# Two token tiles transposed by the DMA, their first two products interleaved, and z spread by a row in DRAM

## The chip, the cores and the metric

The kernel runs on one core of a Trainium2 chip. The time is that of one execution on the device, in microseconds; what is given for a kernel is the median of several executions. An execution is also recorded by the profiler once: that record has a span (first to last instruction), engine busy times, and waits. PE is the matmul engine, DVE the vector engine, ACT the activation engine, POOL the general one; SP issues most DMAs.

## What is computed

For 2048 tokens of width D = 640 the output is a gate between a linear attention with 32 heads of width 20 (feature maps: softmax of a projection and of its negative) and a SwiGLU feed-forward net of width 1728.

```python
qkv = x @ wqkv                                   # q, k, v: 32 heads of 20
pq, pk = q @ w_phi, k @ w_phi                    # per head, 20 x 20
phi_q = concat(softmax(pq), softmax(-pq))        # 40 features a head
phi_k = concat(softmax(pk), softmax(-pk))
kv  = einsum("bhsf,bhsd->bhfd", phi_k, v)        # sums over all tokens
z   = einsum("bhsf->bhf", phi_k)
o   = (phi_q @ kv) / (phi_q @ z + 1e-6)
a   = o @ wo
b   = (silu(x @ w_gate) * (x @ w_up)) @ w_down
g   = sigmoid((x * gate_w).sum(-1))
out = g * a + (1 - g) * b
```

## The kernel before, in words

Tokens are cut into 16 tiles of 128 (`NT`), and these into four blocks of four tiles. Every matmul that contracts over D has five steps c = 0..4 of 128 rows. The stages are written as small functions, and a list of their names and arguments, `ORDER` (line 31), gives the order in which they are issued. Each engine runs its own instructions in that order; the class `_Tracker` (line 45) puts a semaphore wait ahead of an instruction wherever it reads or overwrites what another engine or a DMA has still in hand. So a stage's place in the list sets its place on every engine's queue.

The letters of the list:

- `H` (`warm`): matmuls of a tile of ones, with no use but to keep PE active; `NWARM` to a stage.
- `L` (`load_ffn_weights`): the DMAs of the feed-forward and output weights, on SP.
- `X` (`xpose`): the transpose of one token tile, by five PE transposes and a DVE copy from PSUM. It is done for the tiles t < `NPE`, that `load_x` (line 352) brings as they are; the others arrive transposed by the DMA (`dma_start_transpose`, SP). `G`: the gate's weight as an extra column of `wvg`.
- `V` (`vtile`): v of one tile, ten matmuls (five c, two halves of 320 columns) with the weight rows `wvg`, which come in five DMAs, one for each c; ACT copies the result into `v1r` and the gate's sum into `svec`.
- `W` (`wxpose`): PE transposes of one row block of the k weights (`wkn`), copied by DVE into `wT`. `Y` (`w_blocks`): `wbd`, the small matrices w_phi laid out in blocks, made by POOL and DVE. `M` and `R` (`premult`, lines up to 522): k and q weights multiplied by w_phi, six matmuls for each row block, into `wqk`.
- `K` (`ktile`): pk of a tile, ten matmuls; two exponentials on ACT, sums and reciprocals on DVE, the product on POOL into `ekr`. `E` (`kvtile`): eleven matmuls of `ekr` with v, summed over all tiles in PSUM banks 6 and 7. `I` and `N` begin and end that time: between them three PSUM pairs go round (`next_pair`), outside them four. `N` also runs `kv_finish` (line 525).
- `Z` (`z_broadcast`, line 541): z reaches all partitions. `kv_finish` makes `dz`, a diagonal matrix holding z for each of 11 groups of 120; matmuls with ones spread it to 128 partitions, and ACT copies it into `zb`. `J`: the gates.
- `Q` (`qtile`): pq of a tile and its exponentials `eq`; `A` sums them (`qz`); `B` (`qden`) multiplies them by `zb` (`ez`); `C` (`qscale`) sums that, makes the factors `qc`, and has POOL scale `eq` into `ph`, which a transposing DMA on SP brings to `phiT`.
- `O` (`oitem`, parts 0 to 2 of a block): `phiT` with `kvsb`, matmuls with 64 columns of weights; ACT copies to `oT`.
- `F` (`fitem`, 14 parts of a block): ten matmuls of 512 columns, tanh and a copy on ACT, a step on DVE and one on POOL into `hT`. `D` (`ditem`): 38 matmuls of 320 columns for the output of one tile, from `hT` and `oT`; ACT scales into `osb` and the store goes out. The last tile is done in two halves (line 665).

All of the loads stand ahead of the list, on the queues of SP and ACT (lines 361 to 376). On each queue DMAs are issued one after the other.

Of the kernel before, what the change touches and what calls it, by code (L numbers as in the profile page):

```python
# [6 lines left out]
P = 128  # L7
S_TOK = 2048
D = 640
H = 32  # L10
# [2 lines left out]
NT = S_TOK // P  # L13
NB = 4
NCH = 11
NPE = 4
NV = 6
NWARM = 3
FP = 120 * NCH
FK = FP + 8  # L20
ACTF = mybir.ActivationFunctionType
# [7 lines left out]


ORDER = """
L H0 H1 H2 G H3 H4 H5 X0 H6 H7 V0 X1 X2 X3 V1 Y W0 W1 W2 V2 W3 W4 V3 M0 M1 M2 M3 M4 K0 I V4 K1 R0
K2 V5 K3 E0 R2 V6 K4 E1 K5 R4 E2 K6 E3 V7 K7 R1 E4 V8 E5 K8 K9 V9 F0.0 V10 E6 K10 E7 F0.1 E8 V11
K11 E9 K12 V12 K13 R3 E10 K14 V13 E11 K15 Q0 V14 F0.2 V15 E12 E13 J E14 E15 N Q1 F0.3 Q2 A0 Z A1
B0 A2 F0.4 F0.5 F0.6 C0 B1 F0.7 F1.0 Q3 C1 A3 F0.8 F1.1 B2 F1.2 C2 F0.9 F0.10 B3 Q4 F1.3 A4 Q5 C3
F1.4 F0.11 T F0.12 B4 Q6 C4 A5 F1.5 F1.6 B5 F1.7 O0.0 A6 O0.1 F1.8 B6 Q7 A7 F0.13 O0.2 C5 F1.9
F1.10 Q8 C6 A8 B7 D0.0 D0.1 D0.2 Q9 F1.11 C7 D0.3 F2.0 F2.1 F2.2 F1.12 B8 O1.0 O1.1 O1.2 A9 C8
Q10 F2.3 F1.13 Q11 A10 F2.4 B9 F2.5 C9 A11 B10 Q12 D1.0 F2.6 C10 F2.7 D1.1 F2.8 B11 F2.9 F2.10
Q13 A12 C11 D1.2 Q14 D1.3 O2.0 A13 B12 A14 F3.0 B13 F3.1 F3.2 O2.1 C12 C13 F3.3 F3.4 B14 F2.11
Q15 F2.12 A15 F3.5 F2.13 C14 F3.6 O2.2 B15 F3.7 C15 F3.8 D2.0 F3.9 F3.10 F3.11 F3.12 D2.1 O3.0  # L40
O3.1 O3.2 F3.13 D2.2 D3.0 D3.1 D2.3 D3.2 D3.3
"""


# [143 lines left out]
def _build(nc, A_x, A_wqkv, A_w_phi, A_wo, B_x, B_w_gate, B_w_up, B_w_down, gate_w, out):  # L188
# [5 lines left out]
    def sb(name, shape, dtype):  # L194
        t = nc.alloc_sbuf_tensor(name, list(shape), dtype)
        tr.reg(t, "sbuf", nc.lookup_mloc(t).addr)
        return t
# [14 lines left out]
    hmask = sb("hmask", [P, 3], F32)  # L212
    zt = sb("zt", [P, NCH, 3], F32)
    zf = sb("zf", [P, NCH], F32)
    dz = sb("dz", [P, NCH, 120], BF16)
    zb = sb("zb", [P, FP], BF16)
    svec = sb("svec", [P, NT], F32)
    g2 = sb("g2", [P, NT], F32)
# [22 lines left out]
    def at(name, shape, dtype, rel):  # L241
        n = mybir.dt.size(dtype)
        for s in shape[1:]:
            n *= s
        assert rel + n <= SLAB, (name, rel + n, SLAB)
        t = nc.alloc_sbuf_tensor_at(name, list(shape), dtype, offset=sbase + rel)
        tr.reg(t, "sbuf", sbase + rel)
        return t
# [8 lines left out]
    wph = at("wph", [P, 5, DH], BF16, 28480)  # L257
    bmask = at("bmask", [P, 5, 8], BF16, 28736)
    gwr = at("gwr", [P, P], BF16, 28864)

    ps = nc.alloc_psum_tensor("ps", [P, 8 * 512], F32)
    tr.reg(ps, "psum", 0)

    def bank(b, c0, c1, r0=0, r1=P):
        return ps[r0:r1, b * 512 + c0:b * 512 + c1]
# [66 lines left out]
    def dma(e, dst, src, transpose=False):  # L332
        eo = tr.eng[e]

        def fn():
            if transpose:
                return eo.dma_start_transpose(dst, src)
            return eo.dma_start(dst, src)  # L338
        rd = [src] if src.tensor.name in tr.base else []
        wr = [dst] if dst.tensor.name in tr.base else []  # L340
        return run(e, fn, rd, wr, dma=True)
# [10 lines left out]
    def load_x(t, e="sp"):  # L352
        if t < NPE:
            dma(e, xs[:, t, :], x2[t * P:(t + 1) * P, :])
        else:
            dma("sp", xT[:, t, :, :], x2[t * P:(t + 1) * P, :], transpose=True)

    def load_rows(e, dst, c, c0):
        dma(e, dst, A_wqkv[c * P:(c + 1) * P, c0:c0 + D])

    dma("act", gwr[0:5, :], bass.AP(gate_w.tensor, gate_w.offset, [[P, 5], [1, P]]))
    load_x(0)
    for c in range(5):
        load_rows("sp" if c % 2 else "act", wvg[:, c, 0:D], c, 2 * D)
    load_x(1)
    load_x(2, "act")
    load_x(3)
    dma("act", wph[:, :, :], A_w_phi.rearrange("h e f -> (h e) f").rearrange("(c p) f -> p c f", p=P))
    for c in range(5):
        load_rows("sp", wkn[:, c, :], c, D)  # L370
    for t in range(4, 7):
# [49 lines left out]
    def next_pair():  # L421
        r = ring["i"] % ring["n"]
        ring["i"] += 1
        return r
# [16 lines left out]
        pr = next_pair()  # L441
        mm([(bank(2 * pr, 0, P), ones[:, :], ones[:, :], True, True, False)] * NWARM)

    def vtile(t):
        pr = next_pair()
        pairs = [(bank(2 * pr + hb, 0, 320 + hb), xT[:, t, c, :], wvg[:, c, 320 * hb:640 + hb - 320 * (1 - hb)],
                  c == 0, c == 4, False) for c in range(5) for hb in range(2)]
        if t == 0:
            for c in range(5):
                mm(pairs[2 * c:2 * c + 2])  # L450
        else:
            mm(pairs)
        i = halves(pr).rearrange("p b (h d) -> p b h d", d=DH)
        o = v1v[:, t % NV, 0:H, 0:DH].rearrange("p (b h) d -> p b h d", b=2)
        copy("act", o, i)
        copy("act", svec[:, t:t + 1], bank(2 * pr + 1, 320, 321))

    def head_exps(pr, dst):
        i = halves(pr).rearrange("p b (h d) -> p b h d", d=DH)
# [28 lines left out]
    def kvtile(t):  # L488
# [6 lines left out]
                          t == 0 and jj == 0, t == NT - 1, True))  # L495
        mm(pairs)

    def wxpose(m):
        pr = next_pair()
        o = bankbf(2 * pr, 640)  # L500
        transposes([(o[:, c * P:(c + 1) * P], wkn[:, m, c * P:(c + 1) * P]) for c in range(5)])
        copy("dve", wT[:, m, :, :].rearrange("p c k -> p (c k)"), o)

# [11 lines left out]
    def premult(which, m):  # L515
        pr = next_pair()
        pairs = []
        for i, (hb, c, c0, c1, off) in enumerate(BANDS):
            o = bank(2 * pr + hb, c0 - 320 * hb, c1 - 320 * hb)
            pairs.append((o, (wT if which else wTq)[:, m, c, :], wbd[:, c, off:off + c1 - c0], i in (0, 3), i in (2, 5), True))  # L520
        mm(pairs)
        copy("dve" if which and m % 2 == 0 else "act", wqk[:, which, m, :].rearrange("p (b c) -> p b c", b=2), halves(pr))


    def kv_finish():
        for bk, j0, j1 in ((KV0, 0, 8), (KV0 + 1, 8, NCH)):
            n = j1 - j0
            i = bank(bk, 0, 63 * n, 0, 120).rearrange("p (j h d) -> p j h d", h=3, d=DH + 1)
            tt("dve", zt[0:120, j0:j1, :], i[:, :, :, DH],
               hmask[0:120, :].unsqueeze(1).to_broadcast([120, n, 3]), ALU.mult)  # L530
        reduce(zf[0:120, :], zt[0:120, :, :])
        tt("dve", dz[0:120, :, :], ident[0:120, 0:120].unsqueeze(1).to_broadcast([120, NCH, 120]),
           zf[0:120, :].unsqueeze(2).to_broadcast([120, NCH, 120]), ALU.mult)
        for bk, j0, j1 in ((KV0, 0, 8), (KV0 + 1, 8, NCH)):
            n = j1 - j0
            i = bank(bk, 0, 63 * n, 0, 120).rearrange("p (j h d) -> p j h d", h=3, d=DH + 1)
            for hh in range(3):
                tt("dve", kvsb[0:120, j0:j1, 20 * hh:20 * hh + 20], i[:, :, hh, 0:DH],
                   hmask[0:120, hh:hh + 1].unsqueeze(1).to_broadcast([120, n, DH]), ALU.mult)

    def z_broadcast():
        pr = next_pair()
        dzf = dz[0:120, :, :].rearrange("p j c -> p (j c)")
        mm([(bank(2 * pr, 0, 480), ones[0:120, :], dzf[:, 0:480], True, True, False),
            (bank(2 * pr + 1, 0, 480), ones[0:120, :], dzf[:, 480:960], True, True, False)])
        copy("act", zb[:, 0:960].rearrange("p (b c) -> p b c", b=2), halves(pr, 480))
        pr = next_pair()
        mm([(bank(2 * pr, 0, 360), ones[0:120, :], dzf[:, 960:FP], True, True, False)])
        copy("act", zb[:, 960:FP], bank(2 * pr, 0, 360))

    def gates():
        tsc(svec[:, :], svec[:, :], 60.0, None, ALU.min, ALU.bypass)
# [95 lines left out]
    def ditem(bt, u):  # L648
        buf = bt % 2
        t = 4 * bt + u  # L650
        pr = next_pair()
        tok = slice(P * u, P * u + P)
        ls = [(hT[:, buf, k, tok], wd[:, k, :]) for k in range(13)]
        ls += [(hT[0:104, buf, 13, tok], wd[0:104, 13, :])]
        ls += [(oT[:, buf, m, tok], wog[:, m, :]) for m in range(5)]
        n = len(ls)
        half = [[(bank(2 * pr + hb, 0, 320), l, r[:, 320 * hb:320 * hb + 320], i == 0, i == n - 1, False)
                 for i, (l, r) in enumerate(ls)] for hb in range(2)]
        o = osb[:, t % 4, :]
        if t < NT - 1:  # L660
            mm([p for ab in zip(*half) for p in ab])
            actop(o.rearrange("p (b c) -> p b c", b=2), halves(pr), ACTF.Copy, omg[:, t:t + 1])
            out_evs.append(dma("sp", out2[t * P:(t + 1) * P, :], o))
            return
        for hb in range(2):
            mm(half[hb])
            c = slice(320 * hb, 320 * hb + 320)
            actop(o[:, c], bank(2 * pr + hb, 0, 320), ACTF.Copy, omg[:, t:t + 1])
            out_evs.append(dma("sp", out2[t * P:(t + 1) * P, c], o[:, c]))


    def kv_begin():
# [2 lines left out]
    def kv_end():  # L675
# [1 line left out]
        ring["n"] = 4  # L677

    ops = {
        "H": lambda i: warm(), "X": xpose, "G": gcol, "V": vtile, "W": wxpose,  # L680
        "M": lambda m: premult(1, m), "R": lambda m: premult(0, m),
        "K": ktile, "E": kvtile, "L": load_ffn_weights, "T": tail_weights, "J": gates,
        "Y": w_blocks, "I": kv_begin, "N": kv_end, "Z": z_broadcast,
# [54 lines left out]
```

## Time and profile before

| what | value |
|---|---|
| median of 8 runs | 295.83 us (295.43 to 298.15) |
| the profiled execution's own time | 295.9 us |
| its span | 294.2 us |
| PE busy | 289.1 us, 98% of the span |
| DVE, ACT, POOL busy | 171.7, 148.6, 158.0 us |
| granted PE clock | full over the whole span |
| DMA | 21.28 MB, mean 72 GB/s |

The profile's lines name an engine, a line of the code, an operation with what it writes and reads (out<-in), its shape, and how many there are. In the timeline the first two numbers are the start and the time taken, both in us, and a bracket tells how long the engine had been idle and what ended that. Since every matmul passes through one helper, all have line 284, and are told apart by their tiles. PEld is the loading of weights into PE. SPq and ACTq are the queues that issue DMAs.

### The profile page before, as it was taken

What the parts mean: (1) busy time and instruction counts of PE and PEld (TensorE: products, weight loads), DVE (VectorE), ACT (ScalarE), POOL (GpSimd) and SP (SyncE); (2) the same over time, 40 slices, a digit from 0 to 9 for tenths busy, and PEclk for the clock granted to TensorE, in tenths of its full rate; (3) what the DMA queues carried; (4) which work ended last, traced back from release to release, by engine and by line L of the source; (5) the groups of instructions that cost most, each with busy time, mean ns of one, the idle gap of its engine ahead of it and who ended that gap; (6) DMA issues with size and microseconds to landing.
All of it is one profiled execution on the core that took longest, in us unless ns stands there. A gap on an engine that the chain in (4) does not pass through costs nothing.

```text
span 294.2 us, 4908 instructions
## 1 busy us (share of the span) xinstructions
PE 289.1 (98%) x1981; PEld 174.5 (59%) x1981; DVE 171.7 (58%) x250; ACT 148.6 (51%) x252; POOL 158.0 (54%) x118
## 2 busy tenths in 40 slices
PE   7999999999999999999999999999999999999996
PEld 5777766766444544357764456647544455657774
DVE  1558775585979989997042777539259893100000
ACT  1378865784746655852235862353356644262112
POOL 8709887794268878955025384544056976410000
PEclk9999999999999999999999999999999999999999
DMA  7967899500002222203203021230302223000101
GB/s 215 210 115 114 232 359 362 113 3 0 2 0 49 51 49 49 49 2 76 69 22 72 3 49 25 49 71 2 94 0 49 51 49 71 3 22 25 45 22 48
DMA packets 45993, 21.28 MB, mean 72 GB/s; under 512 B 35794, under 2 KB 45970, under 8 KB 45970
## 3 DMA queue, kind: packets, MB, share of 16 engines
q1 hardware_dynamic: 44728, 20.27, 29.0%
q10 hardware_dynamic: 1242, 0.68, 0.8%
q8 instruction: 16, 0.26, 0.4%
q14 instruction: 7, 0.06, 0.1%
HBM read 9.78 MB, written 2.62 MB: 42 GB/s over the span
## 4 chain that ended last, share of the span: by engine, by line
PE 90%; DVE 5%; DMA 2%; ACTq 1%; ACT 1%; issue 0%
PE ps L284 90%; DMA xs<-in_A_x_dram 2%; DVE qw L323 1%; DVE hT L316 1%; PE ps L296 1%; ACTq L338 1%; DVE qw L316 1%; DVE qm L583 1%; DVE qz L323 0%; DVE ez L312 0%; ACT hT L302 0%; DVE qd L326 0%; DVE qc L588 0%; DVE qd L312 0%; ACT osb L302 0%
## 5 line engine op out<-in xcount | busy, mean ns | idle before, releaser
L312 POOL TENSOR_TENSOR hT<-hT,us 128x512 bf16<-128x512 bf16 (+1 forms) x56 | 69.8, 1258 | 62.5 <-DVE hT L316 62.5
L316 DVE SCALAR_TENSOR_TENSOR hT<-hT,ps 128x512 bf16<-128x512 bf16 (+1 forms) x56 | 37.6, 682 | 61.8 <-ACT hT L302 51.0
L284 PE MATMUL ps<-xT,wg 128*128 128x512 bf16 x260 | 64.7, 380 | 0.3 <-DVE hT L316 0.2
L284 PE MATMUL ps<-xT,wu 128*128 128x512 bf16 x260 | 64.6, 380 | 0.0
L284 PE MATMUL ps<-wd,hT 128*128 128x320 bf16 x448 | 63.7, 300 | 0.0
L302 ACT ACTIVATE hT<-ps 128x512 bf16<-128x512 f32 (+2 forms) x60 | 35.8, 596 | 47.0 <-PE ps L284 45.1
L284 PEld LDWEIGHTS ps<-wd,hT 128*128 128x128 bf16 x448 | 43.8, 98 | 17.8
L312 POOL TENSOR_TENSOR ph<-eq,qc 128x1320 bf16<-128x1320 bf16 x16 | 39.3, 2457 | 27.1 <-DVE qc L588 27.1
L284 PE MATMUL ps<-wqk,xT 128*128 128x320 bf16 x320 | 48.4, 299 | 0.1
L312 POOL TENSOR_TENSOR ekr<-ekr,krec 128x1280 bf16<-128x1280 bf16 x16 | 37.3, 2358 | 16.1 <-DVE krec L326 13.9
L284 PEld LDWEIGHTS ps<-xT,wu 128*128 128x128 bf16 x260 | 25.4, 98 | 30.7
L302 ACT ACTIVATE osb<-ps,omg 128x640 bf16<-128x640 f32 (+1 forms) x17 | 12.9, 762 | 58.5 <-PE ps L284 58.5
L284 PEld LDWEIGHTS ps<-xT,wg 128*128 128x128 bf16 x260 | 24.9, 98 | 29.5 <-issue 1.2
L284 PEld LDWEIGHTS ps<-wqk,xT 128*128 128x128 bf16 x320 | 30.4, 98 | 14.0 <-ACT us L302 0.5
L302 ACT ACTIVATE us<-ps 128x512 bf16<-128x512 f32 (+1 forms) x56 | 33.2, 594 | 0.6 <-POOL hT L312 0.5
L323 DVE TENSOR_REDUCE ksum<-ekr 128x64 f32<-128x1280 bf16 x16 | 23.5, 1468 | 14.7 <-ACT ekr L302 14.7
L302 ACT ACTIVATE eq<-ps 128x640 bf16<-128x640 f32 x32 | 22.5, 703 | 15.7 <-POOL ph L312 11.3
L302 ACT ACTIVATE ekr<-ps 128x640 bf16<-128x640 f32 x32 | 22.4, 704 | 8.4 <-PE ps L284 7.9
L284 PE MATMUL ps<-wvg,xT 128*128 128x320 bf16 (+1 forms) x160 | 25.8, 308 | 0.4 <-DMA wvg<-in_A_wqkv_dram 0.4
L284 PE MATMUL ps<-wog,oT 128*128 128x320 bf16 x160 | 24.5, 299 | 0.0
L323 DVE TENSOR_REDUCE qz<-eq 128x64 f32<-128x1280 bf16 x16 | 23.6, 1479 | 1.3 <-ACT eq L302 1.3
L323 DVE TENSOR_REDUCE qw<-ez 128x64 f32<-128x1280 bf16 x16 | 23.6, 1476 | 0.0
(71 smaller groups left out, 196.5 us busy)
## 6 DMA issues: line engine op xcount, KB each, us to landing
out_dram<-osb SPq DMA_DIRECT2D x15, 160.0 KB, 1.8
wd<-in_B_w_down_dram SPq DMA_DIRECT2D x1, 2080.0 KB, 16.9
wkn<-in_A_wqkv_dram SPq DMA_DIRECT2D x5, 160.0 KB, 5.5
wg<-in_B_w_gate_dram SPq DMA_DIRECT2D x1, 800.0 KB, 7.7
wu<-in_B_w_up_dram SPq DMA_DIRECT2D x1, 800.0 KB, 10.5
wog<-in_A_wo_dram SPq DMA_DIRECT2D x2, 375.0 KB, 6.7
wg<-in_B_w_gate_dram SPq DMA_DIRECT2D x1, 720.0 KB, 11.6
wu<-in_B_w_up_dram SPq DMA_DIRECT2D x1, 720.0 KB, 12.1
```

Of the source, the lines that this page charges most:

```text
L284: last = pe.matmul(o, lhsT=l, rhs=r, start=st, stop=sp_, skip_group_check=sk)
L296: last = pe.transpose(o, i, ident[0:k, 0:k])
L302: return run("act", lambda: act.activation(o, i, func, scale=scale), rd, [o])
L312: return run(e, lambda: eo.tensor_tensor(o, a, b, op), [a, b], [o])
L316: return run("dve", lambda: dve.scalar_tensor_tensor(out=o, in0=a, scalar=s, in1=b, op0=op0, op1=op1), rd, [o])
L323: return run("dve", lambda: dve.tensor_reduce(o, i, AX.X, ALU.add), [i], [o])
L338: return eo.dma_start(dst, src)
L583: run("dve", lambda: dve.tensor_tensor(v2(qm[:, s, :]), v2(qw[:, s, :]), qs, ALU.mult), [qw[:, s, :], qz[:, b, :]], [qm[:, s, :]])
```

## The change

Tiles 2 and 3 are brought transposed by the DMA (`NPE` is 2), x1 comes on the ACT queue, and the chunks of `wvg` change queues. A new stage `U` (`vfirst`) does v of the tiles 0 and 1 together: for each c the two matmuls of tile 0 and then those of tile 1. The list is written anew: six `H` of four matmuls stand before it instead of eight of three, `I` stands ahead of the premults, and the O parts of a block stand elsewhere, those of blocks 0 and 2 with no other PE stage between them. Two `W` share a PSUM pair. The copy of a premult for k is in two halves, one on ACT and one on DVE. In `kv_finish` the diagonal matrix is replaced by a copy of z to bf16 (`zfb`, 120 x 11), and `z_broadcast` writes it to a row of 1320 elements in DRAM and reads that row into all 128 partitions, both on SP. The second half of the last tile is stored from ACT's queue.

```diff
--- before.py
+++ after.py
@@ -13,9 +13,9 @@
 NT = S_TOK // P
 NB = 4
 NCH = 11
-NPE = 4
+NPE = 2
 NV = 6
-NWARM = 3
+NWARM = 4
 FP = 120 * NCH
 FK = FP + 8
 ACTF = mybir.ActivationFunctionType
@@ -29,16 +29,16 @@
 
 
 ORDER = """
-L H0 H1 H2 G H3 H4 H5 X0 H6 H7 V0 X1 X2 X3 V1 Y W0 W1 W2 V2 W3 W4 V3 M0 M1 M2 M3 M4 K0 I V4 K1 R0
-K2 V5 K3 E0 R2 V6 K4 E1 K5 R4 E2 K6 E3 V7 K7 R1 E4 V8 E5 K8 K9 V9 F0.0 V10 E6 K10 E7 F0.1 E8 V11
-K11 E9 K12 V12 K13 R3 E10 K14 V13 E11 K15 Q0 V14 F0.2 V15 E12 E13 J E14 E15 N Q1 F0.3 Q2 A0 Z A1
-B0 A2 F0.4 F0.5 F0.6 C0 B1 F0.7 F1.0 Q3 C1 A3 F0.8 F1.1 B2 F1.2 C2 F0.9 F0.10 B3 Q4 F1.3 A4 Q5 C3
-F1.4 F0.11 T F0.12 B4 Q6 C4 A5 F1.5 F1.6 B5 F1.7 O0.0 A6 O0.1 F1.8 B6 Q7 A7 F0.13 O0.2 C5 F1.9
-F1.10 Q8 C6 A8 B7 D0.0 D0.1 D0.2 Q9 F1.11 C7 D0.3 F2.0 F2.1 F2.2 F1.12 B8 O1.0 O1.1 O1.2 A9 C8
-Q10 F2.3 F1.13 Q11 A10 F2.4 B9 F2.5 C9 A11 B10 Q12 D1.0 F2.6 C10 F2.7 D1.1 F2.8 B11 F2.9 F2.10
-Q13 A12 C11 D1.2 Q14 D1.3 O2.0 A13 B12 A14 F3.0 B13 F3.1 F3.2 O2.1 C12 C13 F3.3 F3.4 B14 F2.11
-Q15 F2.12 A15 F3.5 F2.13 C14 F3.6 O2.2 B15 F3.7 C15 F3.8 D2.0 F3.9 F3.10 F3.11 F3.12 D2.1 O3.0
-O3.1 O3.2 F3.13 D2.2 D3.0 D3.1 D2.3 D3.2 D3.3
+H2 H5 H0 H3 H4 H1 L X0 G X1 U V2 W0 W1 W2 V3 I Y W3 M0 W4 M3 M1 M2 M4 K0 K1 V4 K2 K3 V5 E0 V6 K4
+E1 K5 V7 E2 K6 E3 K7 V8 R2 E4 K8 V9 R1 V10 R4 E5 R3 E6 K9 E7 K10 K11 T V11 E8 R0 V12 V13 K12 E9
+K13 F0.0 E10 V14 F0.1 E11 Q0 A0 E12 K14 K15 V15 Q1 E13 F0.2 E14 F0.3 E15 N F1.0 A1 Z F1.1 Q2 J A2
+F0.4 F1.2 B0 B1 C0 F0.5 F1.3 F1.4 F0.6 B2 Q3 C1 A3 F1.5 F0.7 B3 F1.6 F0.8 C2 F0.9 F0.10 Q4 C3
+F0.11 F1.7 F1.8 A4 F0.12 Q5 F0.13 B4 Q6 F1.9 A5 O0.0 C4 O0.1 B5 C5 A6 O0.2 Q7 B6 F1.10 D0.0 F1.11
+A7 D0.1 Q8 B7 C6 C7 D0.2 Q9 A8 B8 C8 Q10 D0.3 F1.12 O1.0 A9 Q11 A10 F2.0 B9 O1.1 O1.2 F2.1 F1.13
+B10 A11 C9 F2.2 F2.3 D1.0 C10 F2.4 F2.5 F2.6 B11 C11 D1.1 Q12 Q13 A12 B12 Q14 F2.7 F2.8 C12 A13
+D1.2 F2.9 D1.3 F2.10 B13 A14 F3.0 F2.11 F2.12 O2.0 B14 O2.1 O2.2 F3.1 F3.2 C13 F3.3 F2.13 Q15 C14
+F3.4 F3.5 A15 B15 C15 F3.6 F3.7 F3.8 F3.9 F3.10 D2.0 F3.11 O3.0 F3.12 F3.13 O3.1 O3.2 D2.1 D2.2
+D3.0 D3.1 D3.2 D2.3 D3.3
 """
 
 
@@ -212,7 +212,7 @@
     hmask = sb("hmask", [P, 3], F32)
     zt = sb("zt", [P, NCH, 3], F32)
     zf = sb("zf", [P, NCH], F32)
-    dz = sb("dz", [P, NCH, 120], BF16)
+    zfb = sb("zfb", [P, NCH], BF16)
     zb = sb("zb", [P, FP], BF16)
     svec = sb("svec", [P, NT], F32)
     g2 = sb("g2", [P, NT], F32)
@@ -258,6 +258,9 @@
     bmask = at("bmask", [P, 5, 8], BF16, 28736)
     gwr = at("gwr", [P, P], BF16, 28864)
 
+    zrow = nc.dram_tensor("zrow", [FP], BF16)
+    tr.reg(zrow, "sbuf", 1 << 26)
+
     ps = nc.alloc_psum_tensor("ps", [P, 8 * 512], F32)
     tr.reg(ps, "psum", 0)
 
@@ -360,12 +363,12 @@
 
     dma("act", gwr[0:5, :], bass.AP(gate_w.tensor, gate_w.offset, [[P, 5], [1, P]]))
     load_x(0)
+    load_x(1, "act")
     for c in range(5):
-        load_rows("sp" if c % 2 else "act", wvg[:, c, 0:D], c, 2 * D)
-    load_x(1)
-    load_x(2, "act")
+        load_rows("act" if c % 2 else "sp", wvg[:, c, 0:D], c, 2 * D)
+    load_x(2)
+    dma("act", wph[:, :, :], A_w_phi.rearrange("h e f -> (h e) f").rearrange("(c p) f -> p c f", p=P))
     load_x(3)
-    dma("act", wph[:, :, :], A_w_phi.rearrange("h e f -> (h e) f").rearrange("(c p) f -> p c f", p=P))
     for c in range(5):
         load_rows("sp", wkn[:, c, :], c, D)
     for t in range(4, 7):
@@ -441,19 +444,30 @@
         pr = next_pair()
         mm([(bank(2 * pr, 0, P), ones[:, :], ones[:, :], True, True, False)] * NWARM)
 
-    def vtile(t):
-        pr = next_pair()
-        pairs = [(bank(2 * pr + hb, 0, 320 + hb), xT[:, t, c, :], wvg[:, c, 320 * hb:640 + hb - 320 * (1 - hb)],
-                  c == 0, c == 4, False) for c in range(5) for hb in range(2)]
-        if t == 0:
-            for c in range(5):
-                mm(pairs[2 * c:2 * c + 2])
-        else:
-            mm(pairs)
+    def v_pairs(t, pr):
+        return [(bank(2 * pr + hb, 0, 320 + hb), xT[:, t, c, :], wvg[:, c, 320 * hb:640 + hb - 320 * (1 - hb)],
+                 c == 0, c == 4, False) for c in range(5) for hb in range(2)]
+
+    def v_out(t, pr):
         i = halves(pr).rearrange("p b (h d) -> p b h d", d=DH)
         o = v1v[:, t % NV, 0:H, 0:DH].rearrange("p (b h) d -> p b h d", b=2)
         copy("act", o, i)
         copy("act", svec[:, t:t + 1], bank(2 * pr + 1, 320, 321))
+
+    def vtile(t):
+        pr = next_pair()
+        mm(v_pairs(t, pr))
+        v_out(t, pr)
+
+    def vfirst():
+
+        prs = [next_pair(), next_pair()]
+        pairs = [v_pairs(t, prs[t]) for t in range(2)]
+        for c in range(5):
+            for t in range(2):
+                mm(pairs[t][2 * c:2 * c + 2])
+        for t in range(2):
+            v_out(t, prs[t])
 
     def head_exps(pr, dst):
         i = halves(pr).rearrange("p b (h d) -> p b h d", d=DH)
@@ -495,9 +509,12 @@
                           t == 0 and jj == 0, t == NT - 1, True))
         mm(pairs)
 
+    wpair = {}
+
     def wxpose(m):
-        pr = next_pair()
-        o = bankbf(2 * pr, 640)
+        if m % 2 == 0:
+            wpair[m // 2] = next_pair()
+        o = bankbf(2 * wpair[m // 2] + m % 2, 640)
         transposes([(o[:, c * P:(c + 1) * P], wkn[:, m, c * P:(c + 1) * P]) for c in range(5)])
         copy("dve", wT[:, m, :, :].rearrange("p c k -> p (c k)"), o)
 
@@ -519,7 +536,11 @@
             o = bank(2 * pr + hb, c0 - 320 * hb, c1 - 320 * hb)
             pairs.append((o, (wT if which else wTq)[:, m, c, :], wbd[:, c, off:off + c1 - c0], i in (0, 3), i in (2, 5), True))
         mm(pairs)
-        copy("dve" if which and m % 2 == 0 else "act", wqk[:, which, m, :].rearrange("p (b c) -> p b c", b=2), halves(pr))
+        if which:
+            copy("act", wqk[:, 1, m, 0:320], bank(2 * pr, 0, 320))
+            copy("dve", wqk[:, 1, m, 320:D], bank(2 * pr + 1, 0, 320))
+        else:
+            copy("act", wqk[:, 0, m, :].rearrange("p (b c) -> p b c", b=2), halves(pr))
 
 
     def kv_finish():
@@ -529,8 +550,7 @@
             tt("dve", zt[0:120, j0:j1, :], i[:, :, :, DH],
                hmask[0:120, :].unsqueeze(1).to_broadcast([120, n, 3]), ALU.mult)
         reduce(zf[0:120, :], zt[0:120, :, :])
-        tt("dve", dz[0:120, :, :], ident[0:120, 0:120].unsqueeze(1).to_broadcast([120, NCH, 120]),
-           zf[0:120, :].unsqueeze(2).to_broadcast([120, NCH, 120]), ALU.mult)
+        copy("dve", zfb[0:120, :], zf[0:120, :])
         for bk, j0, j1 in ((KV0, 0, 8), (KV0 + 1, 8, NCH)):
             n = j1 - j0
             i = bank(bk, 0, 63 * n, 0, 120).rearrange("p (j h d) -> p j h d", h=3, d=DH + 1)
@@ -539,14 +559,10 @@
                    hmask[0:120, hh:hh + 1].unsqueeze(1).to_broadcast([120, n, DH]), ALU.mult)
 
     def z_broadcast():
-        pr = next_pair()
-        dzf = dz[0:120, :, :].rearrange("p j c -> p (j c)")
-        mm([(bank(2 * pr, 0, 480), ones[0:120, :], dzf[:, 0:480], True, True, False),
-            (bank(2 * pr + 1, 0, 480), ones[0:120, :], dzf[:, 480:960], True, True, False)])
-        copy("act", zb[:, 0:960].rearrange("p (b c) -> p b c", b=2), halves(pr, 480))
-        pr = next_pair()
-        mm([(bank(2 * pr, 0, 360), ones[0:120, :], dzf[:, 960:FP], True, True, False)])
-        copy("act", zb[:, 960:FP], bank(2 * pr, 0, 360))
+
+        with nc.allow_non_contiguous_dma(reason="1320 elements to a row"):
+            dma("sp", bass.AP(zrow, 0, [[1, 120], [120, NCH]]), zfb[0:120, :])
+        dma("sp", zb[:, :], bass.AP(zrow, 0, [[0, P], [1, FP]]))
 
     def gates():
         tsc(svec[:, :], svec[:, :], 60.0, None, ALU.min, ALU.bypass)
@@ -662,11 +678,12 @@
             actop(o.rearrange("p (b c) -> p b c", b=2), halves(pr), ACTF.Copy, omg[:, t:t + 1])
             out_evs.append(dma("sp", out2[t * P:(t + 1) * P, :], o))
             return
-        for hb in range(2):
-            mm(half[hb])
-            c = slice(320 * hb, 320 * hb + 320)
-            actop(o[:, c], bank(2 * pr + hb, 0, 320), ACTF.Copy, omg[:, t:t + 1])
-            out_evs.append(dma("sp", out2[t * P:(t + 1) * P, c], o[:, c]))
+        mm(half[0])
+        actop(o[:, 0:320], bank(2 * pr, 0, 320), ACTF.Copy, omg[:, t:t + 1])
+        out_evs.append(dma("sp", out2[t * P:(t + 1) * P, 0:320], o[:, 0:320]))
+        mm(half[1])
+        actop(o[:, 320:D], bank(2 * pr + 1, 0, 320), ACTF.Copy, omg[:, t:t + 1])
+        out_evs.append(dma("act", out2[t * P:(t + 1) * P, 320:D], o[:, 320:D]))
 
 
     def kv_begin():
@@ -677,7 +694,7 @@
         ring["n"] = 4
 
     ops = {
-        "H": lambda i: warm(), "X": xpose, "G": gcol, "V": vtile, "W": wxpose,
+        "H": lambda i: warm(), "X": xpose, "G": gcol, "U": vfirst, "V": vtile, "W": wxpose,
         "M": lambda m: premult(1, m), "R": lambda m: premult(0, m),
         "K": ktile, "E": kvtile, "L": load_ffn_weights, "T": tail_weights, "J": gates,
         "Y": w_blocks, "I": kv_begin, "N": kv_end, "Z": z_broadcast,
```

## Prediction

> **What bounds the kernel now.** I read the page first, its busy line and its chain of waits. PE is the engine busy nearly all the time and nine tenths of the chain.
>
> ```profile
> PE 289.1 (98%) x1981; PEld 174.5 (59%) x1981; DVE 171.7 (58%) x250; ACT 148.6 (51%) x252; POOL 158.0 (54%) x118
> ...
> PE 90%; DVE 5%; DMA 2%; ACTq 1%; ACT 1%; issue 0%
> ```
>
> DVE, ACT and POOL stand at half. Then the waits of PE alone, to see whether anything else holds it back:
>
> ```profile
> PE ps L284 <- DVE ones L330: 1.1, 1, 1.1
> PE ps L284 <- DVE hT L316: 0.5, 2, 0.3
> PE ps L296 <- DMA gwr<-in_gate_w_dram: 0.4, 1, 0.4
> PE ps L284 <- DMA wvg<-in_A_wqkv_dram: 0.4, 1, 0.4
> ```
>
> It waits 2.4 us in 294, nearly all before 7 us. After the first K tile PE has no slack, so time can come only from PE work removed or from the start. The timeline of the first 20 us (start, duration):
>
> ```profile
> 5.01 1.25 PE L284 MATMUL ps<-wvg,xT 128*128 128x320 bf16 x4
> ...
> 6.63 1.44 PE L284 MATMUL ps<-wvg,xT 128*128 128x320 bf16 x6 [0.36 <-DMA wvg<-in_A_wqkv_dram]
> ...
> 7.91 1.25 PE L296 MATMUL ps<-ident,xs 128*128 128x128 bf16 x15
> ...
> 9.02 1.54 PE L284 MATMUL ps<-wvg,xT 128*128 128x320 bf16 x10
> ...
> 11.45 1.27 POOL L312 TENSOR_TENSOR wbd<-wph,bmask 128x160 bf16<-128x160 bf16 x3
> ...
> 14.73 1.89 PE L284 MATMUL ps<-wbd,wT 128*128 128x140 bf16 x30
> ...
> 17.88 1.54 PE L284 MATMUL ps<-wvg,xT 128*128 128x320 bf16 x10
> ```
>
> See two things. V0's ten matmuls stretch from 5.01 to about 7.9, waiting for chunks of wvg, where V1's ten take 1.54. And a matmul is slower at first: with 0.48 for the longest single one (wvg's own view), the four at 5.01 are (1.25 - 0.48)/3 = 0.26 us apart; V1's ten, with 0.30 for one, (1.54 - 0.30)/9 = 0.138. The clock row shows full speed for both.
>
> **What the Trainium skill says.** "TensorE: Matmul & The Clock Gate", section "Part 1: The HAM clock gate", says that the array runs at half rate until a free-running window of about 3.4 us has been busy. The 0.26 against 0.138 agrees. The same page, "Wait — 56ns, not 53.3ns?", gives N/2.4 + 2.5 ns for a warm matmul: 135.8 ns at N = 320, against 0.138 here. "DMA: Bandwidth & Descriptors", section "Rules for kernel authors", says that a strided last dimension becomes one descriptor per element; its "Specifications" say that under 512 B an element is read, changed and written. No store of that kind is in this trace.
>
> **The change, part by part**, against the profiled execution: 294.2 us of span and 1.7 around it, 295.9. The median shown is 295.83, 0.07 lower.
>
> *z by DRAM.* Three matmuls of the dz group leave PE. They start at 74.67 and the next F matmul at 75.23: 0.56 us, wholly on PE. DVE's dz product (1.53) becomes a copy of 11 columns (about 0.2, as the reduction to zf), ACT loses 1.33. Both lie beside PE and are worth nothing there. In their place come two DMAs on SP, the second waiting for the first; nothing is behind them on SP but phiT of tile 0, which needs B0 anyway. The first consumer is B0 on DVE. Between N and B0 the new list puts F1.0, F1.1, Q2, F0.4 and F1.2 on PE: four F at 2.16 (ten matmuls, from 79.55 to 81.71 in the timeline) and one Q at 1.36, 10.0 us. F1.2's tanh and DVE step add 1.5, so DVE comes to B0 some 11.5 us after the last E (its own work till then is less: six kvsb products 1.16, two A at 1.48, four F steps at 0.69, J 0.93, in all 7.8). If zb is later than that, B0 holds DVE, and the F steps queued behind it hold PSUM pairs; but PE can still fill four pairs with F0.5, F1.3, F1.4 and F0.6, to 10.0 + 8.6 = 18.6. B0, B1, C0 (0.82, 0.82, 2.8) and one F step need 5.1 of that, so zb must be there at 13.5. zfb is ready 0.75 after the last E: PE waits only if the trip takes over 12.7 us. The trip: 1320 elements of 2 bytes, about 88 to an engine. From the queue totals, a 256-byte packet takes 25 ns (5141 in 10 to 20 us, 81.2% of 16 engines), a 1280-byte one 69 ns (611 in 0 to 6 us, 44.1%). Lower bound: 1.6 (landing of an 80 KB store) plus 2.3 (fastest landing of a 160 KB load) = 3.9. Upper, an estimate from the page's read-change-write: 88 elements at 138 ns, twice the 69, 12.2, plus 1.6, plus 2.9 for a 330 KB load: 16.7. I take 25 ns: 2.2 + 1.6 + 2.9 = 6.7, hidden, so the part is worth -0.56. Below nothing for the wait is excluded: PE can't gain by it.
>
> *x2 and x3.* Ten PE transposes and two DVE copies (0.49 each) go. Ten transposes are half of the time of X1 to X3's twenty less the stall, at 0.056 each 0.56 us; this is counted under the start. The two transposing DMAs cost SP 1.3 to 1.5 us each to issue, ahead of wkn, whose issue starts near 5.4 instead of 3.15, and everything later on SP is 2.3 us later. x4's V at about 17 sees x4 land near 14; the F weights, issued from 33, meet F0.0 at about 52: hidden.
>
> *The start.* On the ACT queue wvg's chunk 2 (second) reached PE at 6.62, chunk 4 (third) at 7.48, x2 (fourth) at 8.37: 0.87 us a tile. In the changed order ACT carries x1, wvg1, wvg3: about 5.75, 6.62, 7.48; SP carries wvg0, wvg2, wvg4, moved by 5.9 (q1 has 0.70 MB by 6 us, 4.3 tiles), landing near 7. X1 and its copy (0.28 + 0.49 and latencies) make tile 1 ready at about 6.6. From then 18 of the 20 matmuls at 0.138 are 2.5 us, and the eight that need chunks 3 and 4 start at 8.0, when both have landed: V0 and V1 end at 9.1, where the kernel before ended V1 at 10.55. x2 by DMA moves fifth on SP: landing 8.0 to 8.4; x3 8.7 to 9.8; wkn at 0.65 a tile: wkn2 10.5 to 11.5, wkn4 11.8 to 12.8. So V2 (1.4) to 10.5, W0 to W2 (0.84, and 0.2 of waiting) to 11.5, V3 to 12.9. The premults need wbd, done on POOL at 12.72 in both kernels: no wait. But their copies now come in halves on ACT and DVE: ACT has V3's 0.70 + 0.17 first, to 13.95, then five halves at 0.44 (0.70 for 640, less the 0.26 that separates the output's 0.79 from its 0.53): 16.15. K0's last pair follows and K0 ends at 16.4, against 17.88 before: -1.5. Bounds: wbd at 12.72, one premult 0.31, five halves 2.2, last pair 0.3, gives 15.55, -2.3; wkn later by its whole 2.3 us of issue (0.5 more wait) and the array slow until 7.4 (0.4) leave -0.6.
>
> *O parts adjacent.* By the starts of successive matmuls, entering and leaving the 64-column matmuls costs PE about 0.1 us each over N/2.4; eight groups of them become six: -0.4. Of the 0.5 of DVE wait at O0.0 I count nothing, as any list may have such a wait.
>
> *Last half's store on ACT.* SP was free (issue 292.29 after ACT's 292.26), so only a semaphore hop goes: 0. Bounds -0.1 to +0.3, the slower if ACT's first store there starts later.
>
> *The rest of the list.* Same work, new places. I count 0, bounds -0.4 to +0.5, the latter one new wait as large as the largest before. The sum is -0.56 - 1.5 - 0.4 = -2.5: 295.9 - 2.5 = 293.4 for the execution and, to a tenth, for the median.
>
> **The rivals.** *B, the start gives little:* wkn behind two transposes and three PSUM pairs during the premults, or E0 and E1 waiting for POOL's normalised ekr (for: POOL ended K0's ekr at 24.13, 22.6 if all moves by 1.5, and K1, V4, K2, K3, V5 bring PE to E0 at 16.4 + 6.8 = 23.2, a slack of 0.6; against: wkn's issue still precedes its use by 5 us). Front -0.6, Z -0.56, O -0.1: 294.6. *C, all parts give their best:* array at full speed from 4 us since 24 warm matmuls run unbroken, and the DVE wait at O0.0 goes: 295.9 - 2.3 - 0.56 - 0.9 = 292.2. *D, slower:* the 2-byte store. Past 12.7 us each microsecond of trip is one of PE; past 15.2 the kernel is slower than before; at 16.7 it is 4.0 - 2.5 = +1.5: 297.4 for the execution. For it: no such store was seen; against: 40-byte loads of wph caused no such stretch.
>
> **How the numbers follow.** Main case 0.58 (293.4, itself 292.6 to 294.3), B 0.25, C 0.09, D 0.08. A difference of 0.3%, 0.89 us, is about what a measurement can tell: faster means under 294.94. Main and C, and half of B, give 0.80; the rest of B 0.12; D 0.08. The range 292.3 to 295.2 leaves out D, half of C and the end of B.
>
> **What would show it.** K0's last matmul near 16.4; V0 and V1 done near 9; no PE wait at B0 and zb landing within 7 us of zfb; no dz matmuls; SP's wkn issues from 5.4. I am wrong if PE waits for wT, for ez or for ekr by more than 1 us together.

## The result, and the profile after

The changed kernel takes 301.45 us (median of 11 runs, 300.89 to 302.37) against 295.89 for the kernel before in the same series: a ratio of 1.0181, 95% interval 1.016 to 1.0201. It is slower by 1.8% where 293.4 was forecast, and outside the forecast range of 292.3 to 295.2. The profiled execution took 301.43, with a span of 299.7 and a mean PE clock of 0.989.

The page's busy line, its clock row (forty equal slices, in tenths of full speed), and the chain that ended last:

```profile
PE 288.6 (96%) x1968; PEld 174.7 (58%) x1968; DVE 167.7 (56%) x250; ACT 148.3 (49%) x253; POOL 157.1 (52%) x118
...
PEclk9999999999997799999999999999999999999999
...
PE 80%; DVE 8%; DMA 6%; POOL 4%; issue 1%; ACT 1%; POOLq 0%
```

PE is 0.5 us less busy than before, though its busy time now holds some slow matmuls (below), and the span is 5.5 longer. In the chain PE has fallen from 90% to 80%; DMA has risen from 2% to 6%, DVE from 5% to 8%, and POOL has come in with 4%. Two slices have a lower clock. Some of the waits, from the longer to the shorter (who waited for whom: us in total, times, longest):

```profile
DVE ez L315 <- DMA zb<-zrow: 7.9, 1, 7.9
PE ps L287 <- DVE hT L319: 6.2, 2, 5.8
...
PE ps L287 <- DVE ones L333: 1.1, 1, 1.1
...
PE ps L287 <- POOL wbd L315: 0.7, 1, 0.7
```

B0 (ez) waits 7.9 us on DVE for the load of z; PE then waits 5.8 for an F step (hT) that stands behind B0. The chain in order of time gives the trip's two halves (start, duration):

```profile
73.75 0.84 DVE zfb L311
74.58 0.03 DVE kvsb L315
74.61 12.64 DMA zrow<-zfb
87.27 4.25 DMA zb<-zrow
91.51 0.02 issue
91.54 1.56 DVE ez L315 x2
```

The store of 1320 elements takes 12.64 us to complete, the load 4.25. The DMA engines are not busy that long. This is the DMA view of the stretch 74.5 to 87.3 us, 0.32 us to a digit:

```profile
DMA  0005680000060000000000000000000000000000
...
q1 hardware_dynamic: 1335, 0.00, 5.2%
```

The store's packets have gone by 76.5 us (the 6 further on is an instruction fetch). The load is issued at 87.27, when the store is complete, so 10.8 us pass between the last packet and completion. And PE after its wait:

```profile
96.69 2.83 PE L287 MATMUL ps<-wqk,xT 128*128 128x320 bf16 x10 [5.75 <-DVE hT L319]
...
99.31 1.96 PE L287 MATMUL ps<-xT,wg 128*128 128x512 bf16 x5
```

Ten matmuls that take 1.52 elsewhere take 2.83, five that take 1.24 take 1.96: 2.0 us more, at half rate. So 5.75 + 2.0 = 7.8 us are lost at one place. The start, in the timeline, did gain:

```profile
5.90 4.03 PE L287 MATMUL ps<-wvg,xT 128*128 128x320 bf16 x28 [0.31 <-DVE xT L311]
...
13.11 0.48 PE L287 MATMUL ps<-wbd,wT 128*128 128x140 bf16 x6 [0.70 <-POOL wbd L315]
...
15.37 2.89 PE L287 MATMUL ps<-wqk,xT 128*128 128x320 bf16 x20
...
18.10 1.54 PE L287 MATMUL ps<-wvg,xT 128*128 128x320 bf16 x10
19.47 2.20 PE L287 MATMUL ps<-wqk,xT 128*128 128x320 bf16 x15
```

The 28 hold the rest of U and V2 without a gap. K0, K1 and V4 have been issued by 19.47. In the kernel before the same three had been issued by 20.61, where the next stage, R0, begins:

```profile
20.61 0.48 PE L284 MATMUL ps<-wbd,wTq 128*128 128x140 bf16 x6
```

The start has gained 1.14 us.

### The profile page after: what moved, and what is told of

Read it like the earlier page. It is cut to its first block, busy times and chain, and to the rows that moved or that the text cites. A ratio compares the mean times of both kernels' runs of the same rounds, so it can differ in the third digit from the quotient of the medians.

```text
span 299.7 us, 4889 instructions
## 1 busy us (share of the span) xinstructions
PE 288.6 (96%) x1968; PEld 174.7 (58%) x1968; DVE 167.7 (56%) x250; ACT 148.3 (49%) x253; POOL 157.1 (52%) x118
## 4 chain that ended last, share of the span: by engine, by line
PE 80%; DVE 8%; DMA 6%; POOL 4%; issue 1%; ACT 1%; POOLq 0%
PE ps L287 80%; DMA zrow<-zfb 4%; DVE qw L326 2%; DVE hT L319 2%; DMA zb<-zrow 1%; POOL ph L333 1%; DVE ez L315 1%; POOL wog L333 1%; DVE qw L319 1%; DVE qm L599 1%; POOL bmask L347 1%; POOL wbd L315 0%; DVE qd L329 0%; DVE qz L326 0%; ACT hT L305 0%
## 5 line engine op out<-in xcount | busy, mean ns | idle before, releaser
L315 POOL TENSOR_TENSOR hT<-hT,us 128x512 bf16<-128x512 bf16 (+1 forms) x56 | 68.6, 1238 | 46.1 <-DVE hT L319 45.3
L287 PE MATMUL ps<-xT,wg 128*128 128x512 bf16 x260 | 65.4, 383 | 0.5 <-DVE hT L319 0.4
L287 PE MATMUL ps<-wvg,xT 128*128 128x320 bf16 (+1 forms) x160 | 24.4, 300 | 0.3 <-DVE xT L311 0.3
```

Of the source, the lines that this page charges most:

```text
L287: last = pe.matmul(o, lhsT=l, rhs=r, start=st, stop=sp_, skip_group_check=sk)
L315: return run(e, lambda: eo.tensor_tensor(o, a, b, op), [a, b], [o])
```

## The experiments

The theory: the row in DRAM is the whole loss, and its slow part is the completion of 2-byte writes that lie close together. The rivals: the new list or the start lose as well; any row in DRAM is slow.

**1. z by matmul again.** The three matmuls and two ACT copies of the kernel before come back in place of the row.

```diff
-        copy("dve", zfb[0:120, :], zf[0:120, :])
+        tt("dve", dz[0:120, :, :], ident..., zf..., ALU.mult)
-        dma("sp", bass.AP(zrow, 0, [[1, 120], [120, NCH]]), zfb[0:120, :])
-        dma("sp", zb[:, :], bass.AP(zrow, 0, [[0, P], [1, FP]]))
+        ...
```

> The changed kernel with z spread by the three matmuls with ones again (diagonal product on DVE, copies on ACT); all else as changed. Theory 1 (the row in DRAM alone is the loss: 5.9 us of PE wait and about 2 us of half-rate matmuls after it; the rest of the change gains what was forecast without Z): 294.0, that is 301.45 - 8.0 + 0.56, with no PE wait over 1 us and a full clock. Rival 2 (the new list or the start lose too, and hide behind the z wait): 296 or more.

Measured: 296.26, ratio 1.0031 [1.0016, 1.0046]. The wait of 5.75 us is gone, but 294.0 was missed by 2.3. The timeline, of an execution with a clock of 0.994:

```profile
75.98 0.73 PE L284 MATMUL ps<-dz,ones 120*128 120x480 bf16 x3 [1.53 <-DVE dz L312]
77.06 1.73 PE L284 MATMUL ps<-xT,wg 128*128 128x512 bf16 x5 [0.34 <-DVE kvsb L312]
78.58 2.34 PE L284 MATMUL ps<-xT,wu 128*128 128x512 bf16 x5
```

In the new list Z comes one F after the last E, too early for a diagonal product that is ready at 75.9: PE waits. The list had been laid out for a Z without PE. The runs also show the price of the slow clock by itself: the two with a mean clock of 0.994 took 297.9 and 298.0, eight with 1.0 took 296.2 to 296.3 (one 297.4). So the same kernel takes 1.7 us more when the clock falls, about the 0.6% that is missing from the clock, and it doesn't always fall. That the fall follows this wait is seen in the profiled execution alone.

**2. The same with Z behind Q2.** Edit to the list: `F1.0 A1 F1.1 Q2 Z J` in place of `F1.0 A1 Z F1.1 Q2 J`.

> The changed kernel with z by matmul, as in the first experiment, but Z stands behind Q2 in the list instead of ahead of F1.1, so that the matmuls come 3.5 us later. Theory 1' (the first experiment missed 294.0 only because PE came to Z before DVE had the diagonal product ready, 1.7 us of wait, 0.5 more for a PSUM pair, and a slow clock after it): 294.3, no PE wait at Z. Rival 2' (the list has another loss that the matmuls bring to light): 295.5 or more.

Measured: 295.38, ratio 0.9996 [0.9979, 1.0012]: between the two, and nearer to Rival 2'. There is no wait for dz, but one of 1.2 us behind the three matmuls, which take two PSUM pairs; the next F came before a pair was free (DVE's step on F1.1, which held it, ended at 79.57):

```profile
77.79 0.72 PE L284 MATMUL ps<-dz,ones 120*128 120x480 bf16 x3
...
79.67 1.24 PE L284 MATMUL ps<-xT,wg 128*128 128x512 bf16 x5 [1.16 <-issue]
```

So z by matmul costs this list 0.56 us of work and about 1.2 in pairs. It trails experiment 3 by 1.45; as that pays some 0.5 for its own small transpose, 0.2 are left, and no further loss of size shows in the list.

**3. The row, stored in 11 runs of 240 bytes.**

```diff
+        o = bankbf(2 * pr, 120)[0:NCH, :]
+        transposes([(o, zfb[0:120, :])], 120)
+        copy("act", zr[0:NCH, :], o)
-        dma("sp", bass.AP(zrow, 0, [[1, 120], [120, NCH]]), zfb[0:120, :])
+        dma("sp", bass.AP(zrow, 0, [[120, NCH], [1, 120]]), zr[0:NCH, :])
```

> The changed kernel, but z (120 x 11) is first transposed by one small PE matmul and copied by ACT to 11 rows of 120, so that the store to DRAM writes 11 runs of 240 bytes instead of 1320 runs of 2 bytes; the load into 128 partitions is unchanged. Theory 1a (the number of 2-byte writes makes the store slow): store lands within 3 us instead of 12.6, PE wait gone, 293.5. Rival 1b (a store to DRAM that is read back is slow whatever its runs, the receipt being what takes 11 us): the store still takes about 12 us and the time stays near 301.

Measured: 293.93 (293.92 to 293.98), ratio 0.9939 [0.9928, 0.9951]: faster than both kernels, by 0.6% and 2.5%, and Rival 1b (any row in DRAM is slow) falls. SP's issues, the second of which waits for the first store's completion:

```profile
75.67 0.29 SPq L342 DMA_DIRECT2D zrow<-zr  x1
76.89 0.36 SPq L342 DMA_DIRECT2D zb<-zrow  x1
```

The store completes in 1.2 us instead of 12.6. PE's longest wait after the start is 0.4. Against the change that is 7.5 us: the wait (5.75) and the slow clock (2.0), less about 0.5, by the starts of matmuls, for the transpose and PE's short wait for zfb; between 0.2 and 0.3 is left over. The run doesn't tell the number of the writes from how close together they lie, since both changed; experiments 7 and 8 do.

**4. The row as changed, its use later.** In the list B0, B1, C0 stand behind F1.4 and F0.6, and F1.5 and F0.7 ahead of B2 and Q3.

> The changed kernel with the store and load as they are, but in the list B0, B1 and C0 stand behind F1.4 and F0.6, and F1.5 and F0.7 ahead of B2 and Q3, so that nothing needs z until some 18 us after the last E. Theory 1 (only the instruction that waits, and what is queued behind it on DVE, makes the trip cost): PE wait at B0 gone, 293.5 to 294.5, the trip still 17 us. Rival 3 (the trip costs even when it is covered, since the scaled features come later and the first O part waits): 296 or more, with a wait of PE further on.

Measured: 297.88, ratio 1.007 [1.0057, 1.0083]. The store took 14.0 us here. The wait at B0 falls to 0.3 us, and new ones come: PE waits 4.6 us for F steps in all.

```profile
PE ps L287 <- DVE hT L319: 4.6, 4, 3.0
```

The longest, 3.0, ends at 108.2: ACT had been held 4 us for an eq buffer by POOL's late ph, and DVE had two tiles' B and C to make up. Covering the trip recovers 3.6 of 7.5; Rival 3 holds for the rest with this list. (Another list might do better; none was tried.)

**5. The kernel before with the row as changed.** The replaced lines are those of the diff's `kv_finish` and `z_broadcast`, alone.

> The kernel before with its own list and start, only z by the row in DRAM. There PE has Q1, F0.3, Q2 between N and B0, and then four PSUM pairs: 4.9 + 8.6 = 13.5 us, against the trip of 17 and B0, A2 and an F step (3 us) after it. Theory 1: PE waits about 7 us and then runs at half rate for about 4 us (2 lost), less 0.56 for Z: 295.9 + 8.6 = 304.5. Rival 2 (the list, not the row, makes the loss): below 297.

Measured: 306.67, ratio 1.0381 [1.0359, 1.0402]. The list and the start of before with this one part lose 10.9 us. The store took 14.0 here (its load is issued at 86.39, itself at 72.35), PE waited 9.2 and then ran at half rate. The forecast had 12.6 and 7.

**6. The kernel before with the good row,** and Z moved ahead of F0.3.

> The kernel before with its own list and start, z by the transposed row (one small PE transpose, 11 runs of 240 bytes), with Z moved ahead of F0.3 so that the trip of some 5 us is covered. Theory 1: 295.8 - 0.56 + 0.1 = 295.3, so that of the 1.8 us that the version with the transposed row is faster, 0.5 is Z and 1.3 the start and the list. Rival (a row in DRAM costs even when its store is quick): 296 or more.

Measured: 295.6, ratio 0.9998 [0.9981, 1.0014]. The number is below the rival's 296; the 0.5 us looked for is neither shown nor excluded.

**7. and 8. Stores to DRAM by themselves.** In the kernel of experiment 1, ahead of the first phiT, stores of 1320 bf16 ones from SP, each followed by a load that waits for it, so that the load's issue marks completion. Each was seen in one execution.

```diff
+        for k, (src, step) in enumerate(...):
+            dma("sp", bass.AP(probes[k], 0, step), src)
+            out_evs.append(dma("sp", scr[0:1, 0:1], bass.AP(probes[k], 0, [[0, 1], [1, 1]])))
```

> The changed kernel with z by matmul, and between the weights' loads and the first phiT, while SP and the DMA queues are idle, five stores to DRAM of 1320 bf16 ones, each followed by a load of one element that waits for the store, so that the load's issue shows when the store is complete. They are: 1320 runs of 2 bytes packed as in the change; the same 64 bytes apart; the same 512 bytes apart; 120 runs of 22 bytes; 11 runs of 240 bytes. Theory 1c (writes of 2 bytes that share a piece of memory follow one another): packed 12 us, 64 or 512 bytes apart 2 to 4 us, 22 bytes some 3, 240 bytes 2. Rival 1d (each small write costs the same wherever it goes): packed and spread all 12 us, 120 runs about 1 us above 11 runs. The kernel's own time isn't the question: 294 to 296.

> The changed kernel with z by matmul and six stores to DRAM of 1320 runs of 2 bytes, each followed by a load that waits for it, when the weights' loads are through: 32, 16, 8, 4 bytes apart, packed; then eleven runs of one partition, 4 bytes apart, in 64 bytes of its own. Theory 1c (writes that share 64 bytes follow one another, so the time grows with how many share): 32 bytes apart 3 us, 16 some 3.5, 8 some 5, 4 some 8, packed 13; eleven of one partition 5 to 6. Rival 1e (only writes of different partitions[...] hinder one another): the last one 3 us.

SP's issues of the first (pb is a store, scr the load behind it), in the order of the expectation:

```profile
57.87 0.34 SPq L344 DMA_DIRECT2D pb<-ones  x1
73.70 0.23 SPq L344 DMA_DIRECT2D scr<-pb  x1
73.97 0.32 SPq L344 DMA_DIRECT2D pb<-ones  x1
76.77 0.23 SPq L344 DMA_DIRECT2D scr<-pb  x1
...
83.99 0.28 SPq L344 DMA_DIRECT2D pb<-ones  x1
85.19 0.21 SPq L344 DMA_DIRECT2D scr<-pb  x1
```

Packed 15.8 us (weights were still loading at its start), 64 bytes apart 2.8, then 512 bytes apart 3.4, 120 runs of 22 bytes 3.0, 11 runs of 240 bytes 1.2. Of the second:

```profile
61.60 0.32 SPq L344 DMA_DIRECT2D pb<-ones  x1
65.23 0.22 SPq L344 DMA_DIRECT2D scr<-pb  x1
65.49 0.32 SPq L344 DMA_DIRECT2D pb<-ones  x1
69.73 0.22 SPq L344 DMA_DIRECT2D scr<-pb  x1
70.00 0.32 SPq L344 DMA_DIRECT2D pb<-ones  x1
77.13 0.23 SPq L344 DMA_DIRECT2D scr<-pb  x1
77.40 0.32 SPq L344 DMA_DIRECT2D pb<-ones  x1
92.04 0.22 SPq L344 DMA_DIRECT2D scr<-pb  x1
92.31 0.32 SPq L344 DMA_DIRECT2D pb<-ones  x1
100.78 0.22 SPq L344 DMA_DIRECT2D scr<-pb  x1
```

16 bytes apart 3.6 us, 8 apart 4.2, 4 apart 7.1, packed 14.6; eleven of one partition in 64 bytes of their own 8.5 (and 32 bytes apart 4.5, beside the weights' end). All of these have the same number of 2-byte writes. The main claim of Theory 1c holds: at one number of writes, the time grows as they move closer together. Rival 1d (each costs the same) falls by 2.8 against 14.6, Rival 1e (only writes of different partitions) by the 8.5. Nor are the DMA engines busier: by the DMA views the packets took 5.2% of 16 engines over 12.8 us in the changed kernel's packed store and 21.4% over 3.1 us in the store 64 bytes apart, some 10.6 us of one engine both times.

What the stretch is that they must not share was not settled. A count by 64 bytes is not enough: eleven writes in 64 bytes took 8.5, where 5 to 6 was expected, and sixteen (4 bytes apart) took 7.1. In both a write's neighbour is 4 bytes away, but in the one all eleven come from one partition; the order in which the writes go out may count as well, and wasn't tried.

**9. and 10. x2 and x3 on PE,** in the version of experiment 3.

```diff
-NPE = 2
+NPE = 4
-X1 U V2 W0 W1 W2 V3 I
+X1 U X2 V2 W0 W1 W2 X3 V3 I
```

> The version with the transposed row (11 runs of 240 bytes; 293.93), but x2 and x3 come as they are, x2 on the ACT queue and x3 on SP, and PE transposes them (X2 ahead of V2, X3 ahead of V3): ten PE transposes and two DVE copies come back, and two transposing DMAs leave SP. Theory 4 (PE waits 0.87 us for POOL's wbd ahead of the first premult, so PE work saved ahead of that is hidden): 293.9 to 294.1, the wait for wbd shorter by 0.5. Rival 5 (what is taken off PE counts, as the prediction summed it): 294.5.

Measured: 298.24, ratio 1.0088 [1.0065, 1.011], outside both. PE waited for a chunk of wvg, U ran at little more than half rate (16 matmuls in 3.93 us, where 0.138 apart would be 2.4), and V2 and V3 waited for DVE's copies of their tiles, since they follow them directly:

```profile
5.07 1.39 PE L288 MATMUL ps<-wvg,xT 128*128 128x320 bf16 x4
6.92 3.93 PE L288 MATMUL ps<-wvg,xT 128*128 128x320 bf16 x16 [0.46 <-DMA wvg<-in_A_wqkv_dram]
```

The edit was a poor test, so it was repeated with `U X2 X3 W0 V2 W1 W2 V3`:

> As the run with x2 and x3 transposed on PE (298.24), but X2, X3 and W0 stand ahead of V2, so that PE doesn't come to V2 and V3 before DVE has copied their transposes (0.75 and 1.1 us of wait there). Theory 7 (the misplaced X2 and X3 cost 1.9 us; the rest is slow matmuls in U and a later chunk of wvg, because the plain loads of x2, x3 and wkn fill the engines that bring wvg): 296.4, U still at half rate past 9 us. Rival 4 (only the list was at fault): 294.0 to 294.5.

Measured: 296.3, ratio 1.0034 [1.0017, 1.005], with runs from 295.3 to 298.5 where experiment 3 had 293.92 to 293.98. The number is Theory 7's, but what was to show it, a U at half rate, isn't there: the profiled execution is the quickest of these (295.3), and its U ran at full rate. In it K0 began at 15.80 against 15.30, and by the starts of matmuls PE waited 1.0 us at Z for a PSUM pair where experiment 3 waited 0.3 there. So in the quickest case x2 and x3 by DMA are worth 0.5 us in the start, and 0.7 more at Z, which may be no more than the order in which the PSUM pairs come round in this list. What makes the other runs slower was not recorded, and stays open.

**11. wbd earlier,** in the version of experiment 3: POOL's `memset` of `ph` moves behind the three wbd products.

> The version with the transposed row, but POOL clears ph (3.6 us) behind its three wbd products instead of ahead of them, so that wbd is ready some 3.6 us sooner. Theory 4: the 0.87 us of PE wait ahead of the first premult goes, 293.1. Rival 6 (the premults' copies on ACT, or the k weights' arrival, end later anyway): 293.7 to 293.9.

Measured: 293.69 (293.38 to 295.62), ratio 0.9935 [0.9911, 0.9958]. The wait for wbd went; in the profiled execution x1 and a chunk of wvg came later, and U with them. The 0.2 against experiment 3 is inside the intervals: Rival 6 by its number, inconclusive.

**12. The last half stored from SP,** in the version of experiment 3.

> The version with the transposed row, the second half of the last tile stored from SP again. Theory (a semaphore hop alone): within 0.1 us of 293.93. Rival (the two stores of the last tile follow one another on one queue): 294.3.

Measured: 293.98, ratio 0.9944 [0.9925, 0.9963], against 293.93: nothing, as expected.

## Why the prediction was wrong, point by point

**The trip of z: the failed step is "I take 25 ns: 2.2 + 1.6 + 2.9 = 6.7, hidden".** The first hop took 12.64 us, not 3.8; the second 4.25, not 2.9. The value was chosen from the time that a packet occupies a DMA engine, and that was the wrong quantity: the engines were through after 2 us, and 10.8 us passed until completion. The bounds, 3.9 to 16.7, all but held the 16.9, but by luck: the upper one charged every small element a read and a write of its own, and 1320 elements as small, 64 bytes apart, were complete in 2.8 us (experiment 7). "DMA: Bandwidth & Descriptors", section "Anatomy of one DMA — SWDGE (gpsimd) path", says that most of a DMA's fixed time is the target memory's write receipt, in its words "This can cause a surprisingly long delay especially when the write target is HBM." The section is on another path, as these stores went out from SP's queue, but the direction agrees: 1.2 us to completion for 240-byte runs, and 10.8 us after the last packet for packed 2-byte ones. That these 10.8 us are the receipt is likely and not shown. The page has nothing of how close together the writes lie, which experiments 7 and 8 show to be what counts. With a bound on either side and no row near it, 0.08 for rival D was too little.

**The point from which it decides** was placed well: zb had to be there 13.5 us after the last E. E15 ended at 72.31, B0 began at 91.54, 19.2 after it; the difference, 5.7, is PE's wait of 5.75. But the trip's allowance of 12.7 was short of that by the start: zfb was stored 2.3 us after the last E and not 0.75. DVE had F0.3's step first, and the cast to zfb took 0.84 and not about 0.2. It ran beside a step of POOL and ended with it (74.59 and 74.55); in experiment 6, with POOL idle, it took 0.17. Whether POOL held it up was not tested.

**The price past it** was one term short. "TensorE: Matmul & The Clock Gate", section "Part 1: The HAM clock gate", was cited for the start; it also says that an idle window of about 3.4 us brings the array back to half rate. The prediction didn't apply that to its own wait: after 5.75 us without a matmul PE ran at half rate here, 2.0 us more. Rival D, at 297.4, lacked these 2.0, the 1.6 of the late store and 0.2 of trip: together 301.2. The rest, 0.2 to 0.3, is what the other parts fell short of their sum.

**The start** had the right mechanism, and less of it: 1.14 us instead of 1.5. V0 and V1 ended before 9 as forecast and wkn's issues began at 5.36. But PE was ready for the premults at 12.4 and waited 0.7 for wbd, which POOL had at 12.97; the prediction had PE arrive at 12.9, after it. (Its count of the transposes of X1 to X3 is wrong too: they are fifteen, as its own line shows, and not twenty. Nothing in the sum rests on that.)

**Z off PE, the O parts, the store.** Experiment 3 has all of the change but the small runs, and is 1.8 to 2.0 us faster than before where 2.5 was summed: 1.14 of start, 0.56 for Z less some 0.5 for the transpose and its wait, and 0.6 to 0.8 left for the O parts and the list (0.4 and 0 in the sum). The 0.4 was miscounted: O0.0 and O0.1 already stood together on PE before, with only a wait between them, so seven groups became six, which is 0.2 at the prediction's own rate. PE's wait for DVE at O0.0, two pieces of 0.5 and 0.2 by the starts of matmuls, isn't in the new list, and the prediction counted nothing for it. How the 0.6 to 0.8 divide was not measured. The store was nothing, as forecast.

## What to carry to other kernels

Small stores to DRAM have a price that no engine's busy time shows; price one by the time to its completion, and where elements of a few bytes would lie side by side in DRAM, transpose on chip first and store whole runs. A wait put on an engine that frees another's buffers is worth what is queued behind it, so reckon the moment at which the last buffer is full, and add the half-rate matmuls when PE stands still for some microseconds. And where the bounds of an unseen cost reach past that moment, the chance of the bad case is not small.

## What the runs showed of the hardware

What makes a store of small elements slow is how close together they lie in DRAM. 1320 writes of 2 bytes are complete in 2.8 us when 64 bytes apart, and in 12.6 to 15.8 (five stores) when packed. Against those 2.8, the excess is 0.8 us at 16 bytes apart, 1.4 at 8, 4.3 at 4, and 11.8 packed (by the 14.6 of experiment 8); 32 bytes apart, with other loads still running, gave 1.7. In experiment 1 a wait of PE of 1.9 us, in two parts with three matmuls between, was followed by half rate in the profiled execution, and by the mean clock two of eleven executions lost it, a difference of 1.7 us between runs.
